# Norms kept with tokens on partitions, prefix products scanned once, attention chunks two steps apart

## The chip, the cores and the metric

The kernel runs on one core of a Trainium2 chip. A core has five engines that this text names: PE (TensorE, the matrix engine, with its weight loads as PEld), DVE (VectorE), ACT (ScalarE), POOL (GpSimd) and SP (SyncE, which here only issues DMAs). Each engine takes its instructions in the order in which the program gives them and waits on semaphores. The metric is the device time of one execution in microseconds (us), lower is better.

## The reference, cut to what matters

The input goes through a chunked linear attention, a gated feed-forward layer with a norm, and a second feed-forward layer. All is float32.

```
log_a = np.log(np.clip(a, 1e-06, 1.0))               # a: (4, 8, 768)
...
cum = np.cumsum(la, axis=-1)
L = np.exp(cum[:, :, :, None] - cum[:, :, None, :]) * causal
y_intra = np.einsum('bhij,bhjd->bhid', CB * L, xc)   # CB = C B^T in the chunk
y_inter = np.einsum('bhin,bhnd->bhid', Cc, state) * np.exp(cum)[..., None]
state = decay_full * state + np.sum(Bx, axis=2)
...
rms = np.sqrt(np.mean(x * x, axis=-1, keepdims=True) + 1e-06)   # x: (3072, 256)
xn = x / rms * rms_g
g, val = xn @ w_gate, xn @ w_val                     # 256 -> 1536
x = (g / (1 + np.exp(-g)) * val) @ w_out             # 1536 -> 256
h = x @ w_in                                         # 256 -> 2048
return (h * np.clip(h + 3, 0, 6) / 6) @ w_out2       # 2048 -> 256
```

## The kernel before, in words

The kernel works in chunks of 128 positions: 4 batches times 6 chunks are 24 calls of `attention`. Four chunks, one of each batch, make a block of 512 tokens, and there are six blocks. Phase A sends each block through the first feed-forward layer in 12 steps f (`step("A", ...)`), phase B sends the same tokens through the second in 16 steps. A float32 product is made of three matmuls of rounded parts (`mm3`: high by high, low by high, high by low), so a step of phase A is 12 matmuls of 128x512 into `hps` and 6 into `acc`, a step of phase B 6 and 6.

While PE works on block j, the attention of block j+1 is woven in between its steps. The table `AT` says behind which step f of block j the four chunks of block j+1 and their norm stand in the program. `P.op` collects all operations with their costs, and `Plan.run` puts them in an order by a list schedule with these costs; from then on each engine has a fixed order. Tiles have fixed numbers of buffers; the PSUM tiles "w" (two banks each) rotate over three buffers and are shared by `hps`, the scores and outputs of a chunk (`sps`) and the norm (`rps`).

A chunk: SP loads `cb` (x, B, C), `L` (the decays a of the chunk, spread over partitions) and `P` (the decays, laid out by state rows). DVE scans `L` into running products (`scan`, L347) and `P` likewise (`pscan`, L364). PE makes scores (`score`, L389), DVE multiplies by the decays (`decay`, L398, tile SM), PE makes the outputs (`inner`, L414 to L428), DVE the new state (`state`, L436, tile V), ACT the squares (`square`, L452, tile sq) and a copy of the outputs (`evac`, tile xT).

The norm: the mean of squares over 256 features is a sum over partitions, so PE makes it. For block 0 there is `mean` (L459), two matmuls of a chunk's squares with a column of ones, which leaves the sum of each token on the token's own partition, and `keep` (L465), which stores it. For blocks 1 to 5 there is `sums` (L492) behind the last chunk: eight matmuls with 32 columns of ones, which leave the sums spread over 128x128. From there DVE takes an integer guess of 1/sqrt and three Newton steps (`guess` L501 to L507, `newton` L522 to L524, 13 instructions on 128x128). `back` (L531) spreads the result over all partitions with four matmuls on PE, DVE scales xT (`scale`, L537), and `split` makes the high and low parts that the next block's matmuls need.

The weights arrive as raw float64 bits and are converted on the chip (`weights`, L587 to L616), w1 in 12 tiles during block 0, w2 in 16 tiles after the last norm, since w2's tiles use memory that the attention gives back.

Of the kernel before, what the change touches and what calls it, by code (L numbers as in the profile page):

```python
# [24 lines left out]
AT = {0: 0, 2: 1, 5: 2, 7: 3, 9: 4}  # L25
# [142 lines left out]
def block_kernel(ctx, tc, comb, ablk, w1, w2, cst, out):  # L168
# [28 lines left out]
    ones = ap1.tile([128, 32], F32, name="ones")  # L197
    sel = ap1.tile([128, 4, 128], F32, name="sel")
# [51 lines left out]
    def setup():  # L250
        dve.memset(zero, 0.0)
        dve.memset(ones, 1.0)
        dve.memset(half, 0.5)
        act.activation(out=spare, in_=ones[:, 0:1], func=AF.Sqrt)
# [10 lines left out]
    aclip = dram.tile([NK, H * CH], F32, name="aclip")  # L265
    azero = dram.tile([NK, H * CH], F32, name="azero")
    ac = ap1.tile([96, 2, CH], F32, name="ac")
    az = ap1.tile([96, 2, CH], F32, name="az")

# [10 lines left out]
    P.op({"DVE": 2 * d2(256) + 100}, clip_all, r=[("ac", 0)], w=[("ac", 0), ("az", 0)], boost=1e9)  # L280

    def later():
# [3 lines left out]
        P.op(dma(98304), lambda e: nc.sync.dma_start(out=rows(aclip), in_=ac), r=[("ac", 0)],  # L286
             w=[("aclip", 0)], boost=1e4)
# [14 lines left out]
    def attention(k, j, i):  # L302
# [14 lines left out]
        def ld_P(e):  # L317
            T["P", k] = t = ap3.tile([128, CH], F32, tag="P", name="P")
            src = aclip[k].rearrange("(h i) -> h i", i=CH)
            for h in range(H):  # L320
                nc.sync.dma_start(out=t[h * N:(h + 1) * N], in_=src[h].partition_broadcast(N))  # L321
# [4 lines left out]
        else:  # L326
            P.op(dma(393216), lambda e: ld_cb(e, 0, 768), w=[("cb", k, 0), ("cb", k, 1)],
                 boost=bst)
            P.op(dma(65536), ld_P, r=[("aclip", 0)], w=[("P", k)], boost=bst)
# [31 lines left out]

        def pscan(e):
            t = T["P", k]
            dve.tensor_tensor_scan(out=t, data0=t, data1=zero, initial=1.0,  # L364
                                   op0=ALU.mult, op1=ALU.add)

# [9 lines left out]
        if not first:  # L376
            P.op({"DVE": ds(128)}, pscan, r=[("P", k)], w=[("P", k)], boost=bst)
# [101 lines left out]
        if not j:  # L479
            P.op({"PE": 400}, mean, r=[("sq", j, i)], w=y[:1], boost=bst)  # L480
            P.op({"DVE": 70}, keep, r=y[:1], w=[("rn", j, i)], boost=bst)


    def norm(j, b):
# [3 lines left out]
        def sums(e):  # L488
            r = bank2(wn, "rps")
            for t in range(2):  # L490
                for q in range(B):
                    pe.matmul(out=r[32 * q:32 * q + 32, 0, :CH], lhsT=ones,  # L492
                              rhs=T["sq", j][:, t, q * CH:(q + 1) * CH], start=t == 0,
                              stop=t == 1, skip_group_check=True)


        def guess(e):
            T["rn", j] = v, y, z = [ap1.tile([128, CH], F32, tag=u, name=u)
                                    for u in ("rv", "ry", "rz")]
# [18 lines left out]
        def newton(e):  # L520
            v, y, z = T["rn", j]
            dve.tensor_tensor(out=z, in0=v, in1=y, op=ALU.mult)  # L522
            dve.tensor_tensor(out=z, in0=z, in1=y, op=ALU.mult)  # L523
            dve.scalar_tensor_tensor(out=y, in0=z, scalar=1.5, in1=y, op0=ALU.add, op1=ALU.mult)  # L524


        def back(e):
            r = bank2(wn, "rbc")
            y = T["rn", j][1]
# [10 lines left out]
        wn = nxt(nw)  # L540
        if j:
            P.op({"PE": 80 * 2 * B}, sums, r=[("sq", j, q) for q in range(B)], w=[("w", wn, 0)],
                 boost=bst)
            P.op({"DVE": 4 * d2(CH) + 520}, guess, r=[("w", wn, 0)], w=[("rn", j, -1)],
                 boost=bst)
        else:
            P.op({"ACT": 100}, root, r=[("rn", j, q) for q in range(B)],
                 w=[("rn", j, -1)], boost=bst)
            P.op({"DVE": 150}, invert, r=[("rn", j, -1)], w=[("rn", j, -1)], boost=bst)
        for _ in range(3 if j else 1):  # L550
# [277 lines left out]
```

## Time and profile before

| | us |
|---|---|
| median of 3 runs | 715.87 (714.93 to 718.4) |
| profiled execution, its own time | 718.82 |
| span of its instructions | 717.0 |
| granted TensorE clock over the span | 0.974 of full speed |

The rows further down come from the profiled execution, whose clock starts at its first instruction. The 1.8 us between span and time are start and end outside the instructions.

### The profile page before, as it was taken

What the parts mean: (1) busy time and instruction counts of PE and PEld (TensorE: products, weight loads), DVE (VectorE), ACT (ScalarE), POOL (GpSimd) and SP (SyncE); (2) the same over time, 40 slices, a digit from 0 to 9 for tenths busy, and PEclk for the clock granted to TensorE, in tenths of its full rate; (3) what the DMA queues carried; (4) which work ended last, traced back from release to release, by engine and by line L of the source; (5) the groups of instructions that cost most, each with busy time, mean ns of one, the idle gap of its engine ahead of it and who ended that gap; (6) DMA issues with size and microseconds to landing.
All of it is one profiled execution on the core that took longest, in us unless ns stands there. A gap on an engine that the chain in (4) does not pass through costs nothing.

```text
span 717.0 us, 10364 instructions
## 1 busy us (share of the span) xinstructions
PE 676.3 (94%) x4052; PEld 530.6 (74%) x4052; DVE 364.6 (51%) x503; ACT 295.4 (41%) x491; POOL 300.0 (42%) x249
## 2 busy tenths in 40 slices
PE   8969889997999799979989898999999999999997
PEld 7857667775777677766768776788888888888886
DVE  5898896647354644553255778632233322332232
ACT  3354532222232222222323656744545445454452
POOL 3273543422232242223222456545455455554453
PEclk9998999998999999989999999999999999999999
DMA  6746411130113013201010333100000000000000
GB/s 203 244 178 205 138 56 51 61 89 23 55 56 110 3 56 102 66 2 52 1 59 31 122 113 108 40 1 0 31 1 29 1 0 30 1 31 1 26 4 30
DMA packets 18321, 43.21 MB, mean 60 GB/s; under 512 B 4160, under 2 KB 8032, under 8 KB 18272
## 3 DMA queue, kind: packets, MB, share of 16 engines
q1 hardware_dynamic: 18272, 42.55, 17.9%
q8 instruction: 32, 0.52, 0.3%
q14 instruction: 17, 0.14, 0.1%
HBM read 39.19 MB, written 3.34 MB: 59 GB/s over the span
## 4 chain that ended last, share of the span: by engine, by line
PE 71%; DVE 15%; ACT 4%; issue 3%; DMA 3%; SPq 3%; POOL 1%; DVEq 0%; POOLq 0%; ACTq 0%
PE hps L644 37%; PE acc L644 25%; PE sps L428 2%; DVE cv L609 2%; SPq L321 2%; PE sps L422 2%; PE sps L389 2%; DVE rz L522 1%; PE rps L531 1%; DVE cv L604 1%; POOL gl L241 1%; DVE L L347 1%; DMA yT<-w 1%; DMA L<-azero 1%; DVE rz L523 1%
## 5 line engine op out<-in xcount | busy, mean ns | idle before, releaser
L241 POOL TENSOR_TENSOR gl<-p,gh 128x512 fp32r<-128x512 f32 x162 | 218.1, 1348 | 307.8 <-ACT gh L687 296.2
L682 DVE SCALAR_TENSOR_TENSOR p<-p,hps 128x512 f32<-128x512 f32 x96 | 66.0, 687 | 167.7 <-ACT p L674 167.7
L687 ACT CAST gh<-p 128x512 fp32r<-128x512 f32 x168 | 104.4, 622 | 112.9 <-PE acc L644 100.6
L644 PE MATMUL hps<-xh,w1h 128*128 128x512 f32 x288 | 95.8, 415 | 3.2 <-DVE p L680 3.0
L674 ACT ACTIVATE p<-hps,half 128x512 f32<-128x512 f32 x96 | 66.0, 687 | 79.6 <-POOL gl L241 78.7
L644 PE MATMUL hps<-xh,w1l 128*128 128x512 f32 x288 | 92.1, 402 | 0.0
L644 PE MATMUL hps<-xl,w1h 128*128 128x512 f32 x288 | 91.2, 398 | 0.0
L680 DVE TENSOR_TENSOR p<-p,hps 128x512 f32<-128x512 f32 x72 | 49.1, 682 | 78.9 <-ACT p L672 78.7
L672 ACT ACTIVATE p<-hps 128x512 f32<-128x512 f32 x72 | 43.0, 597 | 96.2 <-PE hps L644 73.8
L644 PE MATMUL acc<-gh,w2h 128*128 128x512 f32 x192 | 74.7, 389 | 0.0
L644 PE MATMUL acc<-gl,w2h 128*128 128x512 f32 x192 | 74.7, 389 | 0.0
L644 PE MATMUL acc<-gh,w2l 128*128 128x512 f32 x192 | 74.7, 389 | 0.0
L644 PEld LDWEIGHTS hps<-xh,w1h 128*128 128x128 f32 x288 | 53.4, 196 | 19.5 <-DVE p L680 5.9
L644 PEld LDWEIGHTS hps<-xh,w1l 128*128 128x128 f32 x288 | 56.1, 195 | 12.5
L644 PEld LDWEIGHTS hps<-xl,w1h 128*128 128x128 f32 x288 | 55.8, 194 | 13.0 <-DVE xl L241 0.4
L644 PE MATMUL hps<-xh,w2h 128*128 128x512 f32 x192 | 60.2, 395 | 3.6 <-DVE p L680 2.7
L644 PE MATMUL hps<-xh,w2l 128*128 128x512 f32 x192 | 59.3, 390 | 0.0
L644 PE MATMUL hps<-xl,w2h 128*128 128x512 f32 x192 | 59.2, 389 | 0.0
L644 PE MATMUL acc<-gh,w1h 128*128 128x512 f32 x144 | 59.0, 410 | 0.0
L644 PE MATMUL acc<-gh,w1l 128*128 128x512 f32 x144 | 56.5, 392 | 0.0
L644 PE MATMUL acc<-gl,w1h 128*128 128x512 f32 x144 | 56.1, 389 | 0.0
L347 DVE TENSOR_TENSOR_SCAN L<-L,eye 128x1024 f32<-128x1024 f32 x20 | 48.4, 2419 | 4.5 <-DMA L<-azero 4.5
(104 smaller groups left out, 871.3 us busy)
## 6 DMA issues: line engine op xcount, KB each, us to landing
L<-azero SPq DMA_DIRECT2D x20, 512.0 KB, 3.8
raw<-w SPq DMA_DIRECT2D x16, 512.0 KB, 3.3
cb<-comb SPq DMA_DIRECT2D x20, 384.0 KB, 3.5
yT<-w SPq DMA_DIRECT2D x6, 768.0 KB, 5.2
rawx<-w SPq DMA_DIRECT2D x6, 768.0 KB, 6.3
out<-yT SPq DMA_DIRECT2D x12, 256.0 KB, 2.0
P<-aclip SPq DMA_DIRECT2D x160, 8.0 KB, 2.2
cb<-comb SPq DMA_DIRECT2D x8, 192.0 KB, 3.4
```

The lines of the kernel that those rows point to most:

```text
L241: eng[e].tensor_tensor(out=out, in0=a, in1=b, op=op)
L321: nc.sync.dma_start(out=t[h * N:(h + 1) * N], in_=src[h].partition_broadcast(N))
L347: dve.tensor_tensor_scan(out=L, data0=L if src is None else T["w", src][:, t], data1=flat(eye8)[:, c], initial=0.0, op0=ALU.mult, op1=ALU.add)
L389: pe.matmul(out=bank2(ws[p // 2], "sps")[:, p % 2, o * CH:(o + 1) * CH], lhsT=cb[r, 512 + o * CH:512 + (o + 1) * CH], rhs=cb[r, 384:512], ...
L422: pe.matmul(out=o[32 * q:32 * q + 32, :], lhsT=T["Vm", k][32 * p:32 * p + 32, c:c + 32], rhs=T["ch", k][32 * p:32 * p + 32, :], start=True ...
L428: pe.matmul(out=o[32 * q:32 * q + 32, :], lhsT=cb[:, 32 * h:32 * h + 32], rhs=SM[:, h, :], start=first, stop=True, skip_group_check=True)
L644: pe.matmul(out=o, lhsT=a, rhs=c, start=first and i == 0, stop=last and i == len(seq) - 1)
L672: act.activation(out=p[:, :n], in_=T["w", hid][:, 0, :n], func=AF.Silu)
L674: act.activation(out=p[:, :n], in_=T["w", hid][:, 0, :n], func=AF.Relu, scale=1.0 / 6.0, bias=half)
L680: dve.tensor_tensor(out=p, in0=p, in1=h, op=ALU.mult)
L682: dve.scalar_tensor_tensor(out=p, in0=p, scalar=1.0, in1=h, op0=ALU.min, op1=ALU.mult)
L687: act.copy(out=t[:, :n], in_=T["p", i][:, :n])
```

## The change

There are four parts. First, every norm uses `mean` and `keep` behind each chunk; `sums` and the matrix `sel` are gone, and `guess` and `newton` work on 128x4 numbers (one column per chunk), with the running value y in PSUM, in the bank of the norm. The guess is 2 instructions and not 4, a Newton step stays at 3. `back` spreads y by a broadcast column against the identity, as block 0 did before. Second, the running products for `P` are scanned once for all chunks (`prefix`, on 96x256) at the start, and `pscan` is gone. Third, `P` is loaded by one transfer of 64 KB and not by eight of 8 KB. Fourth, `AT` puts the chunks behind steps 0, 2, 4, 6 and the norm behind step 8.

```diff
-AT = {0: 0, 2: 1, 5: 2, 7: 3, 9: 4}
+AT = {0: 0, 2: 1, 4: 2, 6: 3, 8: 4}
...
     def clip_all(e):
-        for t in (az, ac):
-            dve.tensor_scalar(out=t, in0=ac, scalar1=1e-6, scalar2=1.0, op0=ALU.max, op1=ALU.min)
+        dve.tensor_scalar(out=az, in0=ac, scalar1=1e-6, scalar2=1.0, op0=ALU.max, op1=ALU.min)
+        dve.tensor_copy(ah[:, :, 0:1], az[:, :, 0:1])
         dve.memset(az[:, :, 0:1], 0.0)
+
+    def prefix(e):
+        dve.tensor_tensor_scan(out=ac.rearrange("p s i -> p (s i)"),
+                               data0=az.rearrange("p s i -> p (s i)"),
+                               data1=ah.rearrange("p s i -> p (s i)"), initial=0.0,
+                               op0=ALU.mult, op1=ALU.add)
...
-            src = aclip[k].rearrange("(h i) -> h i", i=CH)
-            for h in range(H):
-                nc.sync.dma_start(out=t[h * N:(h + 1) * N], in_=src[h].partition_broadcast(N))
+            src = pref[k].rearrange("(h n i) -> h n i", n=1, i=CH).to_broadcast([H, N, CH])
+            nc.sync.dma_start(out=t, in_=src)
...
-            P.op({"DVE": ds(128)}, pscan, r=[("P", k)], w=[("P", k)], boost=bst)
...
-        if not j:
-            P.op({"PE": 400}, mean, r=[("sq", j, i)], w=y[:1], boost=bst)
-            P.op({"DVE": 70}, keep, r=y[:1], w=[("rn", j, i)], boost=bst)
+        P.op({"PE": 550}, mean, r=[("sq", j, i)], w=y[:1], boost=bst)
+        P.op({"DVE": 110}, keep, r=y[:1], w=[("rn", j, i)], boost=bst)
...
         def guess(e):
-            T["rn", j] = v, y, z = [ap1.tile([128, CH], F32, tag=u, name=u)
-                                    for u in ("rv", "ry", "rz")]
+            v, y = T["rn", j][0], bank2(wn, "rps")[:, 0, 0:B]
...
+        def newton(e, end):
+            r = T["w", wn]
+            (v, u, z), y = T["rn", j], r[:, 0, 0:B]
+            dve.scalar_tensor_tensor(out=z, in0=v, scalar=-0.5, in1=y, op0=ALU.mult, op1=ALU.mult)
             dve.tensor_tensor(out=z, in0=z, in1=y, op=ALU.mult)
-            dve.scalar_tensor_tensor(out=y, in0=z, scalar=1.5, in1=y, op0=ALU.add, op1=ALU.mult)
+            dve.scalar_tensor_tensor(out=u if end else y, in0=z, scalar=1.5, in1=y,
+                                     op0=ALU.add, op1=ALU.mult)
...
             for q in range(B):
-                pe.matmul(out=r[:, 1, q * CH:(q + 1) * CH], start=True, stop=True,
-                          lhsT=sel[:, q] if j else y[:, q:q + 1].to_broadcast([128, 128]),
-                          rhs=y if j else eye8[:, 0])
+                pe.matmul(out=T["w", wn][:, 1, q * CH:(q + 1) * CH], start=True, stop=True,
+                          lhsT=T["rn", j][1][:, q:q + 1].to_broadcast([128, 128]),
+                          rhs=eye8[:, 0])
```

The costs that the planner holds for these operations change too, and with them the order of all engines. Three places follow. The first is DVE during block 1, from the state of the last chunk of block 2 to the scaling; V is the state, Vm its masked copy, p the gate product of a step, L the scan of a later chunk. Before:

```order
L436 SCALAR_TENSOR_TENSOR V<-V,P,sps 128x64
L241 TENSOR_TENSOR Vm<-V,cs 128x64
L680 TENSOR_TENSOR p<-p,hps 128x512
L347 SCALAR_TENSOR_TENSOR L<-L,eye_114 128x1024
L364 SCALAR_TENSOR_TENSOR P<-P,zero 128x128
L501 TENSOR_SCALAR rv<-rps 128x128
L503 TENSOR_SCALAR ry<-rv 128x128
L505 TENSOR_SCALAR ry<-ry 128x128
L507 TENSOR_SCALAR rv<-rv 128x128
L522 TENSOR_TENSOR rz<-rv,ry 128x128
```

And in the changed kernel, the same place (the rows of `newton` are cut after the first two):

```order
L433 SCALAR_TENSOR_TENSOR V<-V,P,sps 128x64
L240 TENSOR_TENSOR Vm<-V,cs 128x64
L657 TENSOR_TENSOR p<-p,hps 128x512
L462 TENSOR_SCALAR v_1168<-sps 128x1
L351 SCALAR_TENSOR_TENSOR L<-L,eye_113 128x1024
L488 TENSOR_SCALAR rps<-v_1168 128x4
L490 TENSOR_SCALAR rps<-rps 128x4
L503 SCALAR_TENSOR_TENSOR z_1170<-v_1168,rps 128x4
L504 TENSOR_TENSOR z_1170<-z_1170,rps 128x4
```

The scan of `P` has left the place, `keep` (L462) has come in ahead of the scan of L, and the chain behind it is 2 plus 9 rows on 128x4 and not 4 plus 9 on 128x128.

The second place is PE during block 1 of the changed kernel, around the last `mean` (L456) of that block's chunks. L419 and L425 end the outputs of the chunk.

```order
L419 MATMUL sps<-ch,Vm 32x128 x4
L425 MATMUL sps<-SM,cb 32x128 x4
L621 MATMUL hps<-xh,w1h_81 128x512 x2
L621 MATMUL hps<-xh,w1l_93 128x512 x2
L621 MATMUL hps<-xl,w1h_81 128x512 x2
L456 MATMUL sps<-ones,sq 128x1 x2
L621 MATMUL acc<-gh,w1h_76 128x512
L621 MATMUL acc<-gh,w1l_88 128x512
```

`mean` stands six `hps` matmuls behind the chunk's outputs; four more `acc`, 12 `hps` and six `acc` rows follow before `back` (L511), 24 large matmuls in all.

The third place is PE at the same `back` in the kernel before, where the six rows of f = 83 and the eight matmuls of `sums` stood ahead of 18 `acc` matmuls:

```order
L644 MATMUL hps<-xl,w1h_83 128x512 x2
L492 MATMUL rps<-sq,ones 32x128 x8
L644 MATMUL acc<-gh,w1h_77 128x512
...
L644 MATMUL acc<-gl,w1h_79 128x512
L531 MATMUL rps<-ry,sel 128x128 x4
L644 MATMUL hps<-xh,w1h_84 128x512 x2
```

Counted over the whole order in large matmuls from the start, the five `back`s stood behind 162, 372, 588, 804 and 1020 of 2448; in the changed kernel they stand behind 144, 348, 564, 780 and 996.

## Rows read from the trace of the kernel before

**Rows 1.** The page: span, and busy time by engine with its share.

```profile
span 717.0 us, 10364 instructions
...
PE 676.3 (94%) x4052; PEld 530.6 (74%) x4052; DVE 364.6 (51%) x503; ACT 295.4 (41%) x491; POOL 300.0 (42%) x249
```

**Rows 2.** Busy time in stretches: block 0, and the change of phase.

```profile
43.00:110.00 67.00, 55.96 (x418) 39.76 (x417) 61.37 (x72) 32.79 (x50) 34.89 (x25) 0.92 0.39 129
...
378.00:470.00 92.00, 85.83 (x366) 68.25 (x366) 63.39 (x76) 53.43 (x93) 45.13 (x33) 0.99 0.24 80
```

**Rows 3.** Waits, whole span: us in total, times, longest.

```profile
PE rps L531 <- DVE ry L524: 18.7, 5, 4.6
...
DVE P L364 <- DMA P<-aclip: 11.7, 12, 1.8
```

**Rows 4.** Timeline, end of block 1: start us, us, instruction, idle and releaser.

```profile
162.83 2.28 DVE L347 TENSOR_TENSOR_SCAN L<-L,eye 128x1024 f32<-128x1024 f32 x1
...
164.15 0.64 PE L492 MATMUL rps<-sq,ones 128*32 128x128 f32 x16
...
164.73 0.51 PE L644 MATMUL acc<-gh,w1h 128*128 128x512 f32 x1
...
166.47 0.42 DVE L364 TENSOR_TENSOR_SCAN P<-P,zero 128x128 f32<-128x128 f32 x1 [1.35 <-DMA P<-aclip]
...
166.96 3.96 POOL L241 TENSOR_TENSOR gl<-p,gh 128x512 fp32r<-128x512 f32 x3 [6.47 <-DVE P L364]
167.11 1.23 DVE L503 TENSOR_SCALAR ry<-rv 128x128 int32<-128x128 int32 x1
...
172.07 0.29 DVE L523 TENSOR_TENSOR rz<-rz,ry 128x128 f32<-128x128 f32 x1
...
173.73 2.08 PE L531 MATMUL rps<-ry,sel 128*128 128x128 f32 x8 [4.59 <-DVE ry L524]
```

**Rows 5.** The chain that ended last, PE behind the five waits: start, us.

```profile
108.36 1.16 PE rps L531 x8
109.52 8.19 PE hps L644 x36
...
175.80 6.69 PE hps L644 x24
...
242.76 7.07 PE hps L644 x24
...
312.38 6.67 PE hps L644 x24
...
378.34 6.13 PE hps L644 x24
```

**Rows 6.** Busy time behind the wait in block 1; granted clock third from last.

```profile
173.70:178.20 4.50, 4.47 (x15) 3.89 (x16) 2.24 (x4) 1.24 (x2) 0.88 (x1) 0.50 0.00 0
```

**Rows 7.** Timeline, a chunk's end in block 1.

```profile
159.84 0.73 PE L644 MATMUL hps<-xh,w1h 128*128 128x512 f32 x2
...
159.98 0.28 DVE L436 SCALAR_TENSOR_TENSOR V<-V,P,sps 128x64 f32<-128x64 f32 x1 [2.72 <-PE sps L428]
...
160.29 0.38 ACT L452 ACTIVATE sq<-sps 128x256 f32<-128x256 f32 x1 [2.97 <-DVE V L436]
...
160.57 0.37 ACT L245 COPY xT<-sps 128x256 f32<-128x256 f32 x1
```

**Rows 8.** Timeline of block 0's own norm, and its `keep` by form.

```profile
33.26 0.61 PE L459 MATMUL sps<-ones,sq 128*128 128x1 f32 x4 [0.25 <-ACT xT L245]
...
33.73 2.92 PE L293 MATMUL idle<-zero 128*128 128x128 f32 x24
...
36.93 0.16 DVE L524 SCALAR_TENSOR_TENSOR y<-z,y 128x4 f32<-128x4 f32 x1
...
L465 DVE TENSOR_SCALAR v<-sps 128x1 f32<-128x1 f32 x4 | 0.6, 143 | 1.6 <-PE sps L459 1.2 <-ACT w1h L245 0.3
```

**Rows 9.** Timeline of SP: one chunk's eight loads of P.

```profile
160.41 4.56 SPq L321 DMA_DIRECT2D P<-aclip  x8
```

More of the change, by code (lines that the diff above doesn't have):

```diff
@@ L196, in block_kernel @@
     spare = ap1.tile([128, 1], F32, name="spare")
-    ones = ap1.tile([128, 32], F32, name="ones")
-    sel = ap1.tile([128, 4, 128], F32, name="sel")
+    ones = ap1.tile([128, 1], F32, name="ones")
     eye8 = ap1.tile([128, H, CH], F32, name="eye8")
@@ L253, in setup @@
         dve.memset(half, 0.5)
+        pool.memset(ah, 0.0)
         act.activation(out=spare, in_=ones[:, 0:1], func=AF.Sqrt)
@@ L257, in setup @@
                            fill=1.0, base=0, channel_multiplier=-1)
-        pool.memset(sel, 0.0)
-        for q in range(4):
-            pool.memset(sel[32 * q:32 * q + 32, q], 1.0 / 32.0)
     P.op({"POOL": 4000}, lambda e: None, w=[("eye", 0)], boost=1e9)
-    aclip = dram.tile([NK, H * CH], F32, name="aclip")
+    pref = dram.tile([NK, H * CH], F32, name="pref")
     azero = dram.tile([NK, H * CH], F32, name="azero")
@@ L268, in block_kernel @@
     az = ap1.tile([96, 2, CH], F32, name="az")
+    ah = ap1.tile([96, 2, CH], F32, name="ah")
     def rows(t):
@@ L273, in clip_all @@
     def clip_all(e):
[L274 to L275 removed]
+        dve.tensor_scalar(out=az, in0=ac, scalar1=1e-6, scalar2=1.0, op0=ALU.max, op1=ALU.min)
+        dve.tensor_copy(ah[:, :, 0:1], az[:, :, 0:1])
         dve.memset(az[:, :, 0:1], 0.0)
+    def prefix(e):
[3 more added lines that the diff above has]
+                               op0=ALU.mult, op1=ALU.add)
     P.op(dma(98304), lambda e: nc.sync.dma_start(out=ac, in_=rows(ablk)), w=[("ac", 0)],
          boost=1e9)
[L280 removed]
+    P.op({"DVE": d2(256) + 200}, clip_all, r=[("ac", 0), ("eye", 0)], w=[("az", 0)], boost=1e9)
     def later():
@@ L285, in later @@
              w=[("azero", 0)], boost=1e4)
-        P.op(dma(98304), lambda e: nc.sync.dma_start(out=rows(aclip), in_=ac), r=[("ac", 0)],
-             w=[("aclip", 0)], boost=1e4)
+        P.op({"DVE": ds(256)}, prefix, r=[("az", 0)], w=[("ac", 0)], boost=1e4)
+        P.op(dma(98304), lambda e: nc.sync.dma_start(out=rows(pref), in_=ac), r=[("ac", 0)],
+             w=[("pref", 0)], boost=1e4)
     def idle():
@@ L359, in attention @@
                  r=[("L", k), ("eye", 0)], w=[("L", k, 0), ("L", k, 1)], boost=bst)
[L362 to L365, printed above, removed]
         def ch(e):
@@ L540, in norm @@
         wn = nxt(nw)
+        rn, w0 = [("rn", j, q) for q in range(B)], [("w", wn, 0)]
         if j:
[L542 to L545, printed above, removed]
-        else:
[L547 to L550, printed above, removed]
-            P.op({"DVE": 3 * d1(CH if j else 4) + 260}, newton, r=[("rn", j, -1)],
-                 w=[("rn", j, -1)], boost=bst)
-        P.op({"PE": 200 * B}, back, r=[("rn", j, -1)], w=[("w", wn, 1)], boost=bst)
+            P.op({"DVE": 220}, guess, r=rn, w=w0, boost=bst)
+        else:
+            P.op({"ACT": 200}, root, r=rn, w=w0, boost=bst)
+            P.op({"DVE": 110}, invert, r=w0, w=w0, boost=bst)
+        for i in reversed(range(3 if j else 1)):
+            P.op({"DVE": 330}, lambda e, end=i == 0: newton(e, end), r=rn + w0,
+                 w=w0 + [("rn", j, -1)] * (i == 0), boost=bst)
+        P.op({"PE": 350 * B}, back, r=[("rn", j, -1)], w=[("w", wn, 1)], boost=bst)
         for t in range(2):
```

25 lines of the change are left out of this document (4 added, 21 removed).

## The prediction, made before the changed kernel was run

> **What bounds the kernel now.** I read the page first: PE is busy 676.3 us of a span of 717.0 [rows 1], far ahead of DVE's 364.6, so time comes off only where PE waits, runs slowly, or does work that can be left out. The next view is the list of waits. One wait of PE stands out: the matmuls of `back` wait for the last Newton step, five times, 18.7 us in all [rows 3]. The timeline of block 1 shows how it comes about [rows 4]. PE makes the sums at 164.15, then 18 `acc` matmuls, and stands still from 169.14 until `back` starts at 173.73. DVE meanwhile scans L, waits 1.35 us for the transfer of P, scans P (0.42), and then works through the 13 rows of the norm. One of these takes 0.29 us when it runs alone, but 1.23 while POOL works on `gl`. The reader is to see that the chain is long by its number of rows, by that stretching, and by the wait for P ahead of it, and that PE has nothing else in its order to do meanwhile.
>
> The wait has a second price. From 173.70 to 178.20 the granted clock is 0.50, the lower of the two levels, 1.2 GHz [rows 6]; ahead of it PE had been standing still for 4.59 us [rows 4]. Behind the wait of block 0 (3.3 us of the 18.7, since `back` started at 108.36) 36 matmuls took 8.19 us, 0.2275 each, so 24 are 5.46 us. Behind the other four waits 24 took 6.69, 7.07, 6.67 and 6.13 [rows 5]: 1.23, 1.61, 1.21 and 0.67 too much, 4.7 in all. `back` itself took 2.08 in block 1 [rows 4] and again in blocks 3 and 4, and 1.16 where the clock was full [rows 5]: three times 0.92, 2.8 us. The waits cost 18.7 + 4.7 + 2.8 = 26.2 us.
>
> **The change, part by part.**
>
> *The sums go.* From the start of the sums to the next matmul are 164.73 − 164.15 = 0.58 us of PE [rows 4], five times: 2.9 us off.
>
> *A mean comes behind each chunk.* Block 0's own means show the price: 33.73 − 33.26 = 0.47 us to the next matmul [rows 8]. There the neighbours are small idle matmuls. Between large matmuls a change of shape may cost PE a little more, and no row shows this pair; I bound it by 0.47 below and 0.7 above and take 0.6. Twenty chunks (blocks 1 to 5): 12.0 us on, between 9.4 and 14.
>
> *Does the mean wait?* It reads the squares, and in block 0 it was also held by the copy of xT [rows 8]. In block 1 PE goes on to large matmuls at 159.84, and ACT ends the copy at 160.57 + 0.37 = 160.94, 1.10 us later [rows 7]. In the changed order six `hps` matmuls, 6 × 0.2275 = 1.37 us, stand between. So the mean comes about 0.3 us after its data and costs no wait, as long as ACT isn't busy with something else. What is queued behind a late mean is all of PE.
>
> *The chain gets shorter.* Behind the last mean DVE has, by the new order, one gate product still running, `keep` (0.143 [rows 8]), a scan of L (2.28 [rows 4]) and 11 rows on 128x4. Block 0's rows of that size take 0.16 [rows 8], with the handover 0.2, so 2.2 us. No row shows them with an operand in PSUM; `keep`, which reads PSUM, is no slower, so 0.2 is the value I take. The sum: some 0.3 for the product, then 0.14 + 2.28 + 2.2 and 0.2 of handovers, 5.1 us. PE has 24 large matmuls in that time, 5.46 us. The wait thus ends, with 0.3 us to spare. I book 0.2 us a norm for what is left of it, 1.0 in all, and nothing for the clock: a wait of 3.3 us in block 0 was followed by the full clock [rows 5].
>
> The Trainium skill, page "Perfetto Trace Analysis", section "Optimizing Scalar/DVE Operations", speaks against this: it gives VectorE about 60 ns of overhead on SBUF and about 125 on PSUM for each instruction. As an estimate from that page, 11 rows with 65 ns more each are 0.7 us, PE would wait 0.4 us more a norm, and the total would be 2 us above mine. No row here shows a 128x4 instruction on PSUM, and `keep`'s 143 ns does not bear it out.
>
> The stretching is the open cost. The row of 1.23 us and the one of 0.29 differ by 0.94, and four rows so stretched would be 3.8 us, the upper bound. The stretched row works on SBUF tiles alone, the new ones have an operand in PSUM, and `keep`, which has one, stays at 0.143 over four executions; I take 0. The Trainium skill, page "SBUF — State Buffer", section "SBUF: two separate sides", says that GpSimd and a VectorE instruction with two SBUF inputs or in a 2-port mode lock a port pair against each other for a whole instruction. By it the new rows can't be stretched and this bound is 0; for the old rows the trace agrees (1.23 against 0.29).
>
> *P.* Twenty scans of 0.42 [rows 4] leave DVE, and one of 96x256 comes early, while DVE waits for the first matmuls. Their waits for the transfer, 11.7 us [rows 3], go too; what of that reached PE is in the 18.7 already. On SP eight issues took 4.56 us [rows 9]; one takes about an eighth. SP moves past nothing that PE waits for in blocks 1 to 4. All this is booked at zero, hidden by DVE's idle half in those blocks.
>
> *Block 0* is the exception. DVE is busy there 61.4 of 67 us [rows 2], mostly converting w1, and PE waits for it at several places. The norm moves 18 matmuls (4.1 us) forward in PE's order, but all of DVE's conversions still stand ahead of it, so PE reaches its wait earlier than DVE can end it. Against that DVE loses work: five scans of P (2.1) and some 4.6 us of the norm (6.8 in block 1, from 166.89 to 173.7 [rows 4], less 2.2). The new order also gives POOL all low parts of w1, where POOL and DVE can stretch each other. I keep block 0's share of the sum (3.3 + 0.6 − 2.4 = 1.5 us gained) and bound it by 3 lost and 5 gained.
>
> *The chunks two steps apart.* PE's work is the same. The last norm comes behind 996 large matmuls and not 1020, so the conversion of w2, which starts with it, begins 24 × 0.2275 = 5.5 us earlier in PE's order. In 378 to 470 PE made some 366 large matmuls [rows 2], 83.3 us at 0.2275, of 92; of the 8.7 lost, 1.6 are the slow clock above. Of the other 7 an earlier start can give back between none and 5.5; the waits there are DVE's, POOL's and ACT's order in each step more than late tiles, so I take 1.5.
>
> **Sum.** Off: 26.2 + 2.9 + 1.5 = 30.6. On: 12.0 + 1.0 = 13.0. Net 17.6 us. The profiled execution's own 718.82 becomes 701.2. It lies 2.95 above the median of the runs, so the median 715.87 becomes 698.3; I say 698.
>
> **The rivals.**
>
> *Part of the wait stays.* If DVE's new rows are stretched by POOL, or the scan of L ahead of them is (it works on SBUF alone), the chain grows by 1 to 4 us. With 2 us more, PE waits 1.7 us at each `back`, 8.5 less 1.0 booked: 705.8. With 3.8 it waits 3.5, 17.5 us less 1.0, and the 7.5 us of slow clock come back: 722, the whole gain gone. For it: the old chain was so stretched [rows 4]. Against it: no row of POOL touches a PSUM tile in this kernel. I give it 0.18, most of it between 703 and 711.
>
> *The means wait: slower.* Every mean stands in PE's order, so if ACT reaches square and copy late, all of PE stops. The gain is gone when each of the 20 waits 17.6 / 20 = 0.88 us, that is when the copy ends 1.37 + 0.88 = 2.25 us behind the chunk's outputs and not 1.10 [rows 7]. At 1.2 us each it is 698.3 + 24 = 722. For it: in block 0's own norm the mean did wait for that copy [rows 8], and ACT converts weights in the first block. Against it: in blocks 1 to 4 ACT is idle ahead of the square (2.97 us [rows 7]). I give it 0.05.
>
> *No gain in sum.* The changed order of w1 and w2 may cost at both ends what the norms give: block 0 3 lost in place of 1.5 gained, the change of phase 7 worse in place of 1.5 better, and means at 0.7 (2 more) come to 15: 713. For it: in both stretches POOL gets more low parts, or DVE more casts, by the new order. Against it: DVE's total work falls. I give it 0.07.
>
> **How the numbers follow.** My forecast has 0.70, with a range of its own of 690 to 703 (means at 0.47, 2.6 less; change of phase 4 less; block 0 2 less; above, the skill's 2 us and block 0's 3). With the rivals, of which most lies at 703 to 713, the range for 8 in 10 is 689 to 708. A difference under 0.5% (3.6 us) is about what a measurement of this kernel can't tell from none. Faster by more than that, below 712.3, takes the forecast and most of the first and some of the third rival: 0.88. Within it: 0.06. Slower: 0.06.
>
> **What would show it.** In the new profile PE's wait for the last Newton row should be near zero in the list, the clock behind each `back` 1.00 (in blocks 1 to 4), and the 11 rows about 0.2 us apart. Each mean should stand with about 0.6 us to the next large matmul and no wait for ACT. From one `back` to the next, 65.4 us from 108.36 [rows 5] to 173.73 [rows 4], the time should fall by about 4. The prediction is wrong if the means cost 1 us or more, if the chain's rows are long beside POOL's, or if block 0 or the stretch behind the last norm grows by over 5 us.

## The result, and the profile after

The changed kernel takes 688.81 us (686.76 to 688.9) beside 717.13 (714.93 to 718.97) for the kernel before in the same comparison: a ratio of 0.9599, 95% interval 0.9563 to 0.9636, so 4.0% faster. The forecast of 698 (range 689 to 708) had the direction right, and the time fell just below the range. In the profiled executions the gain is 718.82 − 688.82 = 30.0 us (28.3 between the medians), where the sum said 17.6. Executions of one kernel differ, and their granted clock with them: of the kernel before, the fast ones took from 712.91 us at a clock of 0.983 to 724.55 at 0.969. The rest of this document asks where the other 12.4 us came from.

The page of the changed kernel (span; busy time by engine; granted clock in 40 slices), beside [rows 1]:

```profile
span 687.0 us, 10088 instructions
...
PE 668.1 (97%) x4046; PEld 530.3 (77%) x4046; DVE 340.4 (50%) x506; ACT 296.3 (43%) x492; POOL 293.7 (43%) x231
...
PEclk9999999999999999999999999999999999999999
```

PE's busy time fell by 8, the span by 30: most of the gain is PE no longer standing still. The granted clock is at nine tenths or more in every slice of 17 us.

The end of block 1 in the timeline of the changed kernel (start us, duration, instruction), beside [rows 4] and [rows 7]:

```profile
152.06 0.37 ACT L244 COPY xT<-sps 128x256 f32<-128x256 f32 x1
...
152.83 0.50 PE L456 MATMUL sps<-ones,sq 128*128 128x1 f32 x4
...
153.19 0.48 PE L621 MATMUL acc<-gh,w1h 128*128 128x512 f32 x1
...
154.32 0.15 DVE L462 TENSOR_SCALAR v<-sps 128x1 f32<-128x1 f32 x1
154.39 2.28 DVE L351 TENSOR_TENSOR_SCAN L<-L,eye 128x1024 f32<-128x1024 f32 x1
...
155.38 2.38 POOL L240 TENSOR_TENSOR gl<-p,gh 128x512 fp32r<-128x512 f32 x1 [3.39 <-ACT gh L664]
...
156.59 0.15 DVE L488 TENSOR_SCALAR rps<-v 128x4 int32<-128x4 int32 x1
...
158.52 0.39 PE L621 MATMUL acc<-gl,w1h 128*128 128x512 f32 x1
158.54 0.16 DVE L505 SCALAR_TENSOR_TENSOR y<-z,rps 128x4 f32<-128x4 f32 x1
...
158.85 1.13 PE L511 MATMUL rps<-eye,y 128*128 128x128 f32 x8
159.41 1.29 POOL L240 TENSOR_TENSOR gl<-p,gh 128x512 fp32r<-128x512 f32 x1 [1.66 <-ACT gh L664]
```

The mean starts 0.40 us behind the end of the copy and waits for nothing; the next large matmul comes 0.36 us behind its start. The 11 rows take 158.70 − 156.59 = 2.11 us. `back` starts 0.33 us behind the last large matmul, where one large matmul follows another at 0.23. The 4.59 us of [rows 4] are gone, but with no room left: the chain ends just when PE arrives. So it is in three blocks (0.1 us over the usual 0.23 each); in block 0 `back` starts 0.57 us late by the same count, 0.4 of it in the view of waits below, and the last chain ends 2.1 us before PE is there. In the list of waits the row of 18.7 us [rows 3] has become the last of these:

```profile
PE sps L411 <- DVE SM L395: 2.3, 2, 2.0
...
PE rps L511 <- DVE y L505: 0.4, 1, 0.4
```

To place the gain, both traces are cut where PE starts its large matmuls (128x512, into `hps` and `acc`) number 0, 216, 432 and so on, 216 for each block of phase A. Here is the view of busy time for such stretches (length, then PE, PEld, DVE, ACT, POOL, and the granted clock third from last), of the kernel before:

```profile
43.26:124.44 81.18, 70.14 (x524) 50.28 (x523) 69.37 (x82) 36.62 (x58) 40.93 (x30) 0.94 0.34 113
124.44:193.30 68.86, 64.27 (x466) 47.98 (x465) 36.54 (x54) 18.87 (x35) 21.09 (x20) 0.95 0.19 58
...
392.50:449.45 56.95, 51.23 (x218) 39.95 (x217) 43.43 (x50) 34.61 (x62) 29.58 (x22) 1.00 0.33 111
449.45:717.00 267.55, 262.87 (x1153) 215.60 (x1151) 83.90 (x123) 131.38 (x205) 131.68 (x101) 1.00 0.04 14
```

and of the changed one:

```profile
42.19:118.97 76.78, 69.60 (x527) 49.86 (x526) 64.14 (x81) 32.90 (x54) 41.49 (x29) 0.98 0.30 103
118.97:182.69 63.72, 63.31 (x467) 47.95 (x467) 30.80 (x54) 20.05 (x37) 23.34 (x19) 1.00 0.20 67
...
368.61:419.26 50.65, 49.96 (x217) 40.23 (x216) 42.38 (x56) 31.72 (x57) 21.58 (x15) 1.00 0.37 125
419.26:687.00 267.74, 261.89 (x1153) 215.94 (x1151) 83.38 (x117) 132.23 (x206) 129.38 (x101) 1.00 0.03 12
```

| stretch (large matmuls) | before | after | change | the sum said |
|---|---|---|---|---|
| start and block 0 (up to 216) | 124.4 | 119.0 | −5.4 | −1.3 |
| blocks 1 to 4 (216 to 1080) | 268.1 | 249.6 | −18.4 | −14.8 |
| block 5 (1080 to 1296) | 57.0 | 50.7 | −6.3 | −1.5 |
| phase B | 267.6 | 267.8 | +0.2 | 0 |

(The forecast's net of 17.6 is split here by place: block 0 has its wait, sums, means and residual wait; blocks 1 to 4 have all else but the 1.5 for the change of phase.) Three terms are short: the front by 4.1, blocks 1 to 4 by 3.6, block 5 by 4.8 us. The granted clock went to 1.00 in blocks 1 to 4, and in block 0 from 0.94 to 0.98; what that makes of block 0 is worked out further down.

### The profile page after: what moved, and what is told of

Its sections match the earlier page's. It is cut to its first block, busy times and chain, and to the rows that moved or that the text cites. A ratio compares the mean times of both kernels' runs of the same rounds, so it can differ in the third digit from the quotient of the medians.

```text
span 687.0 us, 10088 instructions
## 1 busy us (share of the span) xinstructions
PE 668.1 (97%) x4046; PEld 530.3 (77%) x4046; DVE 340.4 (50%) x506; ACT 296.3 (43%) x492; POOL 293.7 (43%) x231
## 4 chain that ended last, share of the span: by engine, by line
PE 82%; DVE 9%; issue 3%; ACT 2%; POOL 1%; DVEq 0%; ACTq 0%; POOLq 0%
PE hps L621 44%; PE acc L621 31%; PE sps L425 2%; PE sps L419 2%; DVE yT L581 2%; PE sps L386 2%; DVE yT L586 1%; DVE L L351 1%; DVE SM L395 1%; PE rps L511 1%; PE sps L456 1%; DVE p L657 1%; DVE gl L240 1%; DVE cv L586 1%; DVE bh L240 0%
## 5 line engine op out<-in xcount | busy, mean ns | idle before, releaser
L240 POOL TENSOR_TENSOR gl<-p,gh 128x512 fp32r<-128x512 f32 x153 | 210.8, 1378 | 305.1 <-ACT gh L664 298.8
L621 PE MATMUL hps<-xh,w1h 128*128 128x512 f32 x288 | 92.9, 404 | 2.4 <-ACT p L649 1.6
L621 PE MATMUL hps<-xl,w1h 128*128 128x512 f32 x288 | 88.9, 390 | 1.1 <-POOL xl L240 1.1
L621 PE MATMUL hps<-xh,w1l 128*128 128x512 f32 x288 | 89.4, 392 | 0.0
L649 ACT ACTIVATE p<-hps 128x512 f32<-128x512 f32 x72 | 42.9, 596 | 94.5 <-PE hps L621 55.3
L621 PEld LDWEIGHTS hps<-xl,w1h 128*128 128x128 f32 x288 | 54.1, 188 | 13.1 <-POOL xl L240 1.5
L621 PEld LDWEIGHTS hps<-xh,w1h 128*128 128x128 f32 x288 | 51.7, 189 | 16.2 <-issue 3.4
L621 PEld LDWEIGHTS hps<-xh,w1l 128*128 128x128 f32 x288 | 54.4, 189 | 11.8
L351 DVE TENSOR_TENSOR_SCAN L<-L,eye 128x1024 f32<-128x1024 f32 x20 | 49.9, 2495 | 0.0
```

The lines of the kernel that those rows point to most:

```text
L240: eng[e].tensor_tensor(out=out, in0=a, in1=b, op=op)
L351: dve.tensor_tensor_scan(out=L, data0=L if src is None else T["w", src][:, t], data1=flat(eye8)[:, c], initial=0.0, op0=ALU.mult, op1=ALU.add)
L621: pe.matmul(out=o, lhsT=a, rhs=c, start=first and i == 0, stop=last and i == len(seq) - 1)
L649: act.activation(out=p[:, :n], in_=T["w", hid][:, 0, :n], func=AF.Silu)
```

## The experiments

### One part at a time

My first theory was A: the table `AT` is worth more than the 1.5 us booked, since the missing gain of block 5 lies where the table moves the last norm. Against it stood B (the table is worth 1.5, the rest lies elsewhere) and C (it came from P). e1 and e2 change the table in the kernel before and in the changed one:

```diff
-AT = {0: 0, 2: 1, 5: 2, 7: 3, 9: 4}
+AT = {0: 0, 2: 1, 4: 2, 6: 3, 8: 4}
```

> The kernel before with the new AT table alone (chunks behind steps 0, 2, 4, 6, the norm behind step 8). Theory A (the term of the change of phase was too small: the earlier last norm gives back 4 to 6 us of PE's standing still behind the last norm): 711 to 713 us beside 717.1, with the five waits at back still there (about 18 us). Theory B (the table is worth the forecast's 1.5 us, and the missing gain lies in the norm or in P): 715.6 us.

> The changed kernel with the old AT table. Theory A (table worth 4 to 6 us): 693 to 695 us beside 688.8, the loss in the stretch behind the last back. Theory B (1.5 us): 690.3 us, that stretch as short as in the changed kernel.

e3 has the norm of the changed kernel and the rest of the kernel before; e4 is the changed kernel with P's part undone:

```diff
-            src = pref[k].rearrange("(h n i) -> h n i", n=1, i=CH).to_broadcast([H, N, CH])
-            nc.sync.dma_start(out=t, in_=src)
+            src = aclip[k].rearrange("(h i) -> h i", i=CH)
+            for h in range(H):
+                nc.sync.dma_start(out=t[h * N:(h + 1) * N], in_=src[h].partition_broadcast(N))
...
+            P.op({"DVE": ds(128)}, pscan, r=[("P", k)], w=[("P", k)], boost=bst)
```

> The kernel before with the new norm alone (mean and keep behind every chunk, 128x4 rows, y in PSUM); P scanned for each chunk and loaded by eight transfers, old AT table. Theory A (norm 22, table 5, P about 1): 695 us. Rival C (the missing gain came from P: its scans and eight issues gone from block 0): the norm alone gives the forecast's 26.2 + 2.9 - 13.0 = 16 us, 701 us.

> The changed kernel with P as before: scanned for each chunk and loaded by eight transfers. Theory A (P hidden but for its scans in block 0, where DVE is busy nearly all the time): 689 to 691 us beside 688.8. Rival C (P is worth the missing 10 us): 694 to 699 us, with the loss in block 0 (up to the first back behind it).

e10, run later, is the kernel before with P's part alone.

> The kernel before with P's part alone (one scan at the start, one transfer for each chunk). Forecast: P is hidden, 717 us or, by way of the wait for P ahead of the norm's chain (1.35 us and a scan of 0.42 in block 1), up to 1.8 us less at each back: 708 to 717 us. By theory G large matmul 216 starts 2 us earlier than 124.4, block 5 stays at 55 to 57 us.

Measured, with the same cuts in each profiled execution:

| | us | ratio to before (95%) | large matmul 216 at | blocks 1 to 4 | block 5 |
|---|---|---|---|---|---|
| e1, table alone | 715.47 | 0.9947 (0.9916 to 0.9978) | 124.0 | 267.6 | 55.3 |
| e10, P alone | 711.44 | 0.9894 (0.9857 to 0.993) | 123.9 | 259.4 | 58.2 |
| e3, norm alone | 689.71 | 0.9595 (0.9527 to 0.9662) | 119.5 | 249.7 | 50.9 |
| e4, all but P | 688.99 | 0.9595 (0.9537 to 0.9653) | 121.4 | 249.7 | 50.7 |
| e2, all but the table | 687.86 | 0.9576 (0.9513 to 0.9638) | 115.8 | 250.1 | 50.8 |

Theories A and C fall. With the table left out the time is what it was (A: 693 to 695), and block 5 as short; with P left out too. The new norm alone makes all of the gain, where A had 695 and C 701. The table alone shortens block 5 by 1.7 us, which is the 1.5 of the forecast, and the norm alone shortens it by 6.0, which nothing in the forecast gave to the norm. The two do not add up: beside the new norm the table is worth 0.2 us there (50.8 in e2, 50.7 in the changed kernel), so B holds for the kernel before, and its 690.3 for e2 did not come.

P alone does gain, 8.7 us of it in blocks 1 to 4: it takes a wait and a scan out of the old chain, whose rows stay long. In these blocks the waits at `back` are 3.9 us less (11.5 in place of 15.4), and the granted clock is 0.99 in place of 0.96. Over the whole span the view of waits has, for e10, in place of the 18.7 us of [rows 3]:

```profile
PE rps L533 <- DVE ry L526: 14.7, 5, 3.3
```

With the short chain that gain is not there to be had again, as the forecast had it ("what of that reached PE is in the 18.7 already"). Block 5 of e10, at 58.2, is longer than expected, at a granted clock of 0.97.

### Block 5: what the plan believes, or what runs

The norm's code changes two things at once: the instructions, and the costs by which `Plan.run` orders everything. The guess goes from 1051 ns to 220, a Newton step from 858 to 330, `back` from 800 to 1400. Theory D says that block 5 is shorter because of the order that follows from these costs, E because there is less to do. e5 puts the old costs under the new instructions, e6 the new costs under the old ones:

```diff
-            P.op({"DVE": 220}, guess, r=rn, w=w0, boost=bst)
+            P.op({"DVE": 4 * d2(CH) + 520}, guess, r=rn, w=w0, boost=bst)
...
-            P.op({"DVE": 330}, lambda e, end=i == 0: newton(e, end), r=rn + w0,
+            P.op({"DVE": 3 * d1(CH if j else 4) + 260}, lambda e, end=i == 0: newton(e, end), r=rn + w0,
...
-        P.op({"PE": 350 * B}, back, r=[("rn", j, -1)], w=[("w", wn, 1)], boost=bst)
+        P.op({"PE": 200 * B}, back, r=[("rn", j, -1)], w=[("w", wn, 1)], boost=bst)
```

> The changed kernel, with only the planner's costs of the norm set back to the old ones (guess 1051 ns, each Newton step 858, back 800; the instructions are the new ones). Theory D (block 5, large matmuls 1080 to 1296, is 6.3 us shorter because the plan now takes the norm for short and so puts w2's conversion elsewhere in each engine's order): that stretch goes back from 50.7 to 55 or 57 us, the whole to 693 to 695 beside 688.8. Theory E (it is shorter because PE and DVE really have less to do behind the last norm): the stretch stays at 51, the whole at 688 to 690. Blocks 1 to 4 stay within 0.5 us each in both.

> The kernel before, with only the planner's costs of the norm set to the new ones (guess 220 ns, each Newton step 330, back 1400); its 13 rows are as long as before. Theory D (the plan's order): block 5 falls from 56.9 to 51 or 52 us, while the wait at each back grows by up to 2 us, since fewer matmuls are planned ahead of it; in all 715 to 722 us. Theory E: block 5 stays at 55 to 57, in all 717 to 727.

e5 takes 691.86 us (ratio 0.9609, 0.9552 to 0.9666), e6 714.31 (0.994, 0.9903 to 0.9976). Block 5 of e5, new instructions with old costs, in the views of busy time and of waits:

```profile
368.20:423.50 55.30, 51.17 (x218) 39.97 (x217) 40.75 (x47) 34.55 (x62) 31.45 (x23) 1.00 0.34 115
```

```profile
PE hps L621 <- DVE p L657: 4.1, 7, 1.8
```

and of e6, old instructions with new costs:

```profile
394.00:444.80 50.80, 50.12 (x217) 40.15 (x216) 42.14 (x56) 33.00 (x59) 20.23 (x15) 1.00 0.36 125
```

```profile
PE hps L644 <- DVE p L680: 0.5, 2, 0.3
```

Block 5's length goes with the costs and not with the instructions: 55.3 and 57.0 with the old ones, 50.8 and 50.7 with the new, all at the full clock. D holds, E falls. The totals are lower than D had them, 693 to 695 and 715 to 722: of the 4.6 us that block 5 of e5 is longer, phase B gives 0.8 back and blocks 1 to 4 0.5, and in e6 the waits at `back` grow by 1.1 us in blocks 1 to 4 together and not by up to 2 each. What the order does in block 5 is seen in the timeline of the kernel before:

```profile
396.77 3.04 POOL L241 TENSOR_TENSOR gl<-p,gh 128x512 fp32r<-128x512 f32 x2 [3.40 <-PE acc L644]
396.99 1.67 DVE L609 SCALAR_TENSOR_TENSOR cv<-raw,cv 128x512 int32<-128x512 int32 x1
...
398.14 0.60 ACT L672 ACTIVATE p<-hps 128x512 f32<-128x512 f32 x1 [0.92 <-POOL gl L241]
...
398.69 1.40 DVE L247 CAST w2h<-cv 128x512 fp32r<-128x512 f32 x1
...
400.13 0.69 DVE L241 TENSOR_TENSOR w2l<-cv,w2h 128x512 fp32r<-128x512 f32 x1
400.74 0.68 DVE L680 TENSOR_TENSOR p<-p,hps 128x512 f32<-128x512 f32 x1
...
401.47 0.74 PE L644 MATMUL hps<-xh,w1h 128*128 128x512 f32 x2 [2.02 <-DVE p L680]
```

The gate product of this step has its input from ACT at 398.74, but stands on DVE behind two conversions of w2, of which the cast takes 1.40 us here beside POOL's `gl`. It starts at 400.74, and PE's next `hps`, which wants a PSUM buffer back, stands still until it is done, 2.0 us. Seven such waits make 5.7 us in the kernel before, two make 0.5 in the changed one:

```profile
PE hps L644 <- DVE p L680: 5.7, 7, 2.0
...
PE hps L621 <- DVE p L657: 0.5, 2, 0.3
```

The forecast looked at what the table moves here; the costs of the norm move it too, presumably by changing when the plan believes the last norm to be over (no run changes the costs of the last norm alone). Whether this order is better by more than luck is a question of its own (e11 and e12, below). Phase B changes as well, in both directions: its first 48 matmuls take 13.3 us in place of 10.9, and what follows gives 2.3 back: 1.2 in the next 192 matmuls and 0.45 in each of three blocks (43.5 for 192 matmuls in place of 44.0), less 0.2 at the end.

### The chain and the means

e7 makes each Newton step twice in blocks 1 to 5, with the order unchanged:

```diff
         def newton(e, end):
+            if j:
+                once(e, False)
+            once(e, end)
+
+        def once(e, end):
```

> The changed kernel with each Newton step made twice in blocks 1 to 5 (9 rows of about 0.2 us more, 1.76 us; the order is the same). If the chain ends just when PE comes to back (0.1 us of waiting in three blocks, 0.6 in the first, 2.1 us to spare in the last): 1.7 us more in each of four blocks and 0 in the last, 6.8 in all, 695.5 us. If PE has room: under 1 us more. If the waits bring the slow clock back as well: 2 us more for each, 700 us or more.

It takes 695.49 us (ratio 0.9659, 0.9595 to 0.9723); its runs lie at 693.41 to 697.8, and the traced one is the shortest. The waits and the timeline of `back` in it:

```profile
PE rps L516 <- DVE y L510: 6.8, 4, 1.7
```

```profile
157.92 0.39 PE L626 MATMUL acc<-gl,w1h 128*128 128x512 f32 x1
159.99 1.13 PE L516 MATMUL rps<-eye,y 128*128 128x128 f32 x8 [1.68 <-DVE y L510]
160.88 0.48 PE L626 MATMUL hps<-xh,w1h 128*128 128x512 f32 x1
```

Four waits of 1.7 us, none in the last block: the chain does end just when PE arrives, and the 0.3 us to spare of the forecast were none. Blocks 1 to 3 grow by 1.75, 1.74 and 1.73 us; block 0, where the fourth wait lies, keeps its length (76.6 beside 76.8): PE waits 1.2 us more in it, but at a granted clock of 1.00 and not 0.98. Behind a wait of 1.68 us the next matmul comes 0.89 us after `back`, as in the changed kernel (159.73 − 158.85 = 0.88), and the granted clock from 160 to 164 is 1.00.

e8 leaves out the means of two blocks:

```diff
-            for t in range(2):
+            for t in range(0 if j in (1, 3) else 2):
```

> The changed kernel without the means of blocks 1 and 3 (keep reads a column of the squares in their place, so the scale of the outputs of these blocks is wrong; same order). The four means of block 3 lie between large matmuls 432 and 648, the four of block 1 in block 0 (0 to 216), where DVE is busy nearly all the time. Theory F (a mean takes 0.5 us of a busy PE, and in block 0 it takes what PE would have stood still): 2.0 us less in 432 to 648, under 0.7 in 0 to 216, 686 us. By the forecast's price, 0.6 us everywhere: 2.4 less in each, 684 us.

Stretch 432 to 648 falls from 63.6 to 62.8, by 0.8 us and not 2.0, and block 0 by 0.5. The whole, 690.84 us (0.9598, 0.9529 to 0.9667), says nothing at this size. Block 0's 0.5 is within theory F's bound, but it does not show F's reason: beside the changed kernel PE waits 0.6 us more in it, and the granted clock is 0.96 and not 0.98. In the other stretch the miss tells something. Only three of block 3's means lie in it; the first stands ahead of it, behind large matmul 426, and there leaving it out gives nothing: the large matmuls to either side start 1.14 us apart with the mean and without it, since PE waits for ACT's p there, 0.41 us with the mean and 0.75 without. And without the means PE reaches `back` earlier, and the chain on DVE isn't ready. In the timeline of e8:

```profile
221.37 0.39 PE L622 MATMUL acc<-gl,w1h 128*128 128x512 f32 x1
222.16 1.02 PE L512 MATMUL rps<-eye,y 128*128 128x128 f32 x7 [0.40 <-DVE y L506]
```

The 0.79 us from the one to the other are 0.47 more than in the changed kernel. What the means took was in part time that the chain needs anyway; 0.81 and 0.47 are 1.28 us for three means, 0.43 each. Counted in the changed kernel's trace, from a mean's start to the next matmul, the 15 means in blocks 1 to 4 take 7.1 us: twelve take 0.36 each, and three, the first of their blocks, 0.91, with that wait of 0.41 in it. The average is 0.47.

### Block 0: DVE's work, or the order

Theory G: block 0 is bound by DVE, so that work taken from DVE shortens it. Rival H: its waits only fell differently with the new order. e9 adds two idle scans behind the first two `keep` of blocks 1 and 3, order unchanged:

```diff
+            if j in (1, 3) and i < 2:
+                dve.tensor_tensor_scan(out=dummy, data0=flat(eye8), data1=flat(eye8), initial=0.0,
+                                       op0=ALU.mult, op1=ALU.add)
```

> The changed kernel with two idle scans of 128x1024 more on DVE, 2.28 to 3.1 us each, behind the first two keeps of blocks 1 and 3 (into a tile that nobody reads; same order). Theory G (block 0 is bound by DVE's work, so the 4.6 us that the norm takes off DVE there, and the 2.1 of P's scans, come back one for one): large matmul 216 starts 4 to 6 us later than 119.0, the stretch 432 to 648 stays within 0.5 us, 693 to 695 us in all. Rival H (the gain of block 0 came from the changed order and its waits, not from DVE's work): under 1.5 us in block 0, 689 to 690 us.

e9 takes 695.89 us (0.9671, 0.9618 to 0.9724). Large matmul 216 starts at 125.1, 6.1 us later, for two scans of 2.28 us; stretch 432 to 648, where DVE is idle half the time, grows by 1.1, more than I allowed. One of block 3's two scans does that, at 201.3; the other, at 187.1, lies ahead of the stretch, and 216 to 432 keeps its 63.7 us. e13 goes the other way and has ACT make all high parts of w1:

```diff
-        P.op({"ACT": a1(cols), "DVE": d2(cols)}, hi, r=[kt if wide else kr], w=[kh])
+        P.op({"ACT": a1(cols), "DVE": d2(cols)} if tag else {"ACT": a1(cols)}, hi,
+             r=[kt if wide else kr], w=[kh])
```

> The changed kernel with the high parts of w1 made on ACT alone (before, DVE made four of the twelve in block 0, 0.59 us each, 2.4 us; ACT is busy 33 of 77 us there). Theory G (block 0 is bound by DVE's work): large matmul 216 starts 2 to 4 us earlier than 119.0, the rest stays, 685 to 687 us. Rival H (order and waits): within 1 us of 119.0, 688 to 690.

e15 is the changed kernel on the same chip:

> The changed kernel itself, unchanged, on the same chip: 688.8 us, large matmul 216 at 119.0.

e13 takes 685.43 us (0.9564, 0.9529 to 0.9599), e15 688.07 (0.9599, 0.9563 to 0.9635); the runs of e13 lie at 684.13 to 687.28, those of e15 at 686.75 to 689.22. So e13 has the lowest median here, 2.6 us (0.4%) below the changed kernel, though the runs of the two overlap. Large matmul 216 starts at 115.7 beside 119.0, blocks 1 to 5 agree within 0.1 us, and phase B is 0.4 shorter. The busy time of 42 to 119 us in e13:

```profile
42.00:119.00 77.00, 72.33 (x546) 52.46 (x546) 63.56 (x80) 38.21 (x61) 46.76 (x30) 1.00 0.31 106
```

and in e15:

```profile
42.00:119.00 77.00, 69.98 (x530) 50.70 (x528) 64.83 (x81) 33.20 (x55) 41.65 (x29) 0.98 0.30 104
```

PE is busy 2.4 us more in the same window. But the granted clock is 1.00 there and 0.98 here, and in e9 it is lower still:

```profile
42.00:125.00 83.00, 74.02 (x527) 53.17 (x526) 69.48 (x83) 32.94 (x53) 42.75 (x29) 0.92 0.28 95
```

So the clock is a third candidate, which neither G nor H names. As an estimate, a stretch of T us at a mean granted clock c loses up to T × (1 − c) to it. Block 0 (large matmuls 0 to 216), with PE's waits summed from the view of waits (e12 and e14 belong to the next section):

| | length, us | PE's waits | granted clock | lost to the clock, estimate |
|---|---|---|---|---|
| before | 81.1 | 10.9 | 0.94 | 4.9 |
| changed | 76.8 | 7.2 | 0.98 | 1.5 |
| e15, changed again | 76.7 | 7.0 | 0.98 | 1.5 |
| e9, two scans more | 83.0 | 9.0 | 0.92 | 6.6 |
| e13, w1 on ACT | 73.1 | 4.5 | 1.00 | 0 |
| e12 | 73.7 | 5.5 | 1.00 | 0 |
| e14 | 78.5 | 7.2 | 0.96 | 3.1 |

Of the 6.2 us that e9 adds to block 0, 1.8 are waits and most of the rest goes with the clock; of the 3.5 us that e13 takes from that of e15, 2.5 are waits and up to 1.5 the clock. PE's waits follow DVE's work in both, and in this sense G holds in its direction, but not one for one, and the length of block 0 shows the clock as well. The low clock lies in or behind stretches in which PE stood still: in the kernel before it is 0.72 from 48 to 60 us, where PE works 7.78 of the 12 us, in the changed one 0.88 from 84 to 98, where it works 11.62 of 14. Each row is one execution. P alone (e10) moved the end of block 0 by 0.5 us only, and the next run went against G.

### The table again

e11 and e12 set the last norm one step earlier, with two ways to place the chunks; e14 adds the edit of e13 to e12:

```diff
-AT = {0: 0, 2: 1, 4: 2, 6: 3, 8: 4}
+AT = {0: 0, 2: 1, 4: 2, 5: 3, 7: 4}
```

> The changed kernel with the last chunk behind step 5 and the norm behind step 7 (one step, 18 large matmuls, earlier). If the last 4 us of excess at the change of phase come from w2's conversion being late: large matmuls 1080 to 1344 take 61.5 to 63 us and not 64.0, 686 to 688 us. If they come from the order alone: 64.0 and 688.8; with a worse order 692 or more.

> The changed kernel with chunks behind steps 0, 1, 3, 5 and the norm behind step 7. As the run before at the change of phase (61.5 to 63 us for 1080 to 1344 if w2 was late, 64.0 if not); in block 0, where DVE is full, the first two chunks come closer together, which moves work and adds none: large matmul 216 within 3 us of 119.0.

> The same with the chunks behind steps 0, 1, 3, 5 and the norm behind step 7. If less work on DVE and the closer chunks add up: large matmul 216 at 113, 685 us. If both draw on the same slack of DVE: 115.5 as in that kernel without the edit, 688 us.

e11 takes 694.15 us (0.9658, 0.9611 to 0.9704), with block 5 at 56.2; e12 688.13 (0.9564, 0.9522 to 0.9607), with block 5 at 50.7 and large matmul 216 at 115.5. Its large matmuls 1080 to 1344 take 62.3 us, as expected if w2 was late, but its blocks 1 to 4 take 2.9 us more, and its phase B is at 43.9 for 192 matmuls again. An earlier last norm alone gives nothing. In block 5 of e11 PE again waits seven times for gate products, 4.7 us in all, so the new costs do not make block 5 short with every table: the order that comes of both decides. e14 takes 692.48 (0.9654, 0.9615 to 0.9693), with large matmul 216 at 120.5, 5.0 us later than in e12, although the edit is one that shortened block 0 in e13. Block 0 of e14 and of e12:

```profile
41.90:120.50 78.60, 71.29 (x528) 51.25 (x526) 62.44 (x78) 35.99 (x58) 42.99 (x28) 0.96 0.31 101
...
41.80:115.50 73.70, 68.12 (x528) 48.96 (x526) 61.84 (x77) 34.40 (x56) 46.44 (x31) 1.00 0.31 109
```

PE waits 1.7 us more in e14, and up to 3.1 go to the clock. I can't say which place in its order costs that; in block 0 DVE's work, the order and the clock all count, and the runs don't split the 5.4 us of the front between them.

## Why the prediction was too small, by its own steps

**The waits at `back`, their clock, the sums.** Right. In blocks 1 to 4 `back` takes 2.6 us less (forecast 2.8), the sums 2.3 (2.3), and the large matmuls with the waits in them 20.6 (15.4 of waits and 4.7 of slow clock, less 0.8 kept: 19.3). From the first `back` to the second 60.3 us pass in place of 65.4, 1.4 of the difference for six large matmuls fewer between them, so 3.7 us less where about 4 were forecast. The chain was forecast at 5.1 us from a mean's end; in block 1 it takes 5.4 (153.33 to 158.70), since `keep` starts 1.0 us behind the mean and not 0.3. The 0.3 us to spare were none (e7), and the 0.2 booked for each norm covered what was left.

**The means.** Mis-sized, by 9.6 − 7.1 = 2.5 us in blocks 1 to 4. The average of 0.47 is the forecast's lower bound by luck: twelve means took 0.36, below it, and three 0.91, with a wait for ACT that the forecast did not have and that e8 shows, for one of the three, to be there without the mean as well. In block 0 the 2.4 charged may be too much, but e8's 0.5 does not price it, at another clock.

**Block 0.** The step that failed is "all of DVE's conversions still stand ahead of it, so PE reaches its wait earlier than DVE can end it", and with it the term that gave the block its share of the sum and nothing else. The wait at `back` went from 3.3 to 0.4 us, as booked. Beside it PE's waits for SM, 7.6 us in the kernel before, are 2.3 in the changed one:

```profile
PE sps L414 <- DVE SM L398: 7.6, 2, 4.9
```

Other waits of 4.5 us have come in, for ACT, POOL and DVE, so all of PE's waits in the block go from 10.9 to 7.2, 3.7 less where 3.1 were booked. The sum had nothing for the granted clock in this block, which rose from 0.94 to 0.98: by the estimate above up to 3.4 us. The first large matmul also starts 1.1 us earlier, which no run explains. DVE had 5.2 us less to do (69.4 to 64.1 us busy), and PE's waits follow such changes in e9 and e13, but the end of block 0 hardly moves in e10 and moves the wrong way in e14; so how much of the front is DVE's work, how much the order and how much the clock stays open.

**The change of phase.** The step that failed is "so I take 1.5" with the table as the only cause. The table alone gave 1.7 (e1), but beside the new costs it gives 0.2, so the 1.5 is right only for the kernel before. The other 4.6 us of the 6.3 come from the norm's new costs in the plan (e5 and e6), a part of the change that the forecast counted as no term. This is the largest miss. A reading in that step is off too: the 1.6 us of slow clock that it took off the stretch from 378 (0.67 and, it seems, the 0.92 of `back`) hold a `back` that had ended by 378.34 [rows 5]; the clock of 0.99 over these 92 us [rows 2] leaves 0.9, by the same estimate. The rival "no gain in sum" had weighed a changed order in both stretches, but only as a loss.

**The stretching beside POOL.** Right to book none: all 15 rows of L503 and all 15 of L504 took 0.16 us. The Trainium skill, page "Perfetto Trace Analysis", section "Optimizing Scalar/DVE Operations", gives DVE an overhead of about 60 ns for each instruction on SBUF and about 125 on PSUM; these rows with an operand in PSUM take no more than block 0's on SBUF did (0.16, [rows 8]), so the trace does not agree here, and the 2 us that the prediction estimated from that page did not come. The rival "part of the wait stays" did not come about. Of "the means wait" block 0 shows a little: its means wait 1.4 us in all for ACT's squares and copies; in blocks 1 to 4 none waits.

## What to carry to other kernels

Where a list schedule orders the program, an edit's costs are an edit of their own: run the new code under the old costs and the old code under the new ones, and see which of the two the time follows. Price an added instruction by what its engine does in that stretch, not by its own length: here a mean cost 0.43 us where PE was busy (e8) and nothing at the one place tried where PE had to wait for ACT behind it anyway. Before a difference is put down to an engine's work, the granted clock of the stretch belongs beside it: in block 0 it lies between 0.92 and 1.00, and PE's waits alone do not give the lengths. Once a chain ends just when the engine that waits for it arrives, cutting it further gains nothing, and the next gain lies elsewhere, as e13's 2.6 us did.

## What the hardware showed that was not expected

Which engine is stretched differs between the two kernels. With 128x128 rows on SBUF beside POOL's `gl`, DVE's rows grow from 0.29 to 1.37 us (e10's timeline):

```profile
166.37 4.00 POOL L241 TENSOR_TENSOR gl<-p,gh 128x512 fp32r<-128x512 f32 x3 [6.41 <-ACT gh L689]
166.43 1.37 DVE L524 TENSOR_TENSOR rz<-rv,ry 128x128 f32<-128x128 f32 x1
...
170.56 0.29 DVE L524 TENSOR_TENSOR rz<-rv,ry 128x128 f32<-128x128 f32 x1
```

In the changed kernel `gl` starts while the scan of L runs, and it is POOL's row that takes 2.38 us and not 1.29, while the rows with an operand in PSUM stay at 0.16 beside it (they are 128x4 as well, and no run tells the place from the size). The Trainium skill, page "SBUF — State Buffer", section "SBUF: two separate sides", says that whichever of the two starts first keeps the shared port pair for its whole instruction. Both cases agree with that: in e10 `gl` started first, here the scan did, which had 1.29 us to go when `gl` started (the 2.38 us are 0.2 short of these 1.29 and the 1.29 that `gl` takes alone).
